# Identity products ahead of FFN, constants first, and a new order of the first FFN groups, in a fused retention and gated FFN kernel

## The chip, the cores and the metric

One core of a Trainium2 chip. The metric is device time in microseconds (us) for one execution. The kernel before takes 235.17 us in the median of its first 3 runs (234.81 to 235.84); lower is better. All tensors are fp32 in HBM; products run in bf16 with fp32 accumulation.

## The reference

```python
# retention: a decaying state per head; B=4, H=8, S=768, D=64
gamma = 1 - 2.0 ** (-5 - arange(H)); scale = 1 / sqrt(D)
for t in range(S):
    state = gamma * state + einsum('bhd,bhe->bhde', k[:, :, t], v[:, :, t])
    y[:, :, t] = scale * einsum('bhd,bhde->bhe', q[:, :, t], state)
# FFN: 3072 tokens, 512 -> 1536 -> 512
x = y.transpose(0, 2, 1, 3).reshape(B * S, H * D)
out = (1 / (1 + exp(-(x @ w_gate))) * (x @ w_val)) @ w_out
```

## The kernel before

Retention is computed in chunks of 128 tokens; FFN takes them in six blocks of 512 tokens (`xT[t]` is the transposed input of block t). Block 0 needs chunks 0 to 3, which are computed ahead as two "runs" of two chunks each. This opening takes some 27 us; after it, TensorE alternates FFN groups with pieces of later chunks. The schedule is written by hand, which fixes the order of each engine's instructions. Parts:

```python
def load_run(x, a, dtype, eng, name):       # one buffer per name: v's second load (vr) reuses the first's
    t = const.tile([128, H, 2 * D], dtype, name=name, tag=name, bufs=1)
    eng.dma_start(out=t, in_=...)
def scale_v(g, eng):                        # "L189": v times a table
    eng.tensor_tensor(vs[g], vf[g], tabv[...], op=ALU.mult)
def y_out_run(g):                           # "xT": VectorE writes a chunk's columns of FFN's input
    nc.vector.tensor_tensor(xT[0][:, :, cols]..., y[g]..., tab_y(g)..., op=ALU.mult)
def up(t, n1, lo=0, hi=512):                # 4 products with w_gate, 4 with w_val; hT = sigmoid * value
    ...
def keep_on(n):                             # identity products: no use but to keep TensorE busy
    u = bank([128, 512])
    for _ in range(n):
        nc.tensor.matmul(u[:, :128], ident, ident, start=True, stop=True)
# ... (cut) the opening:
scale_run(0, nc.vector)                     # vsr[0] = v * table
vr[1] = load_run(v, 1, F32, nc.sync, "vr")
# ...
keep_on(24)
transpose_run(kr[0], kT[0], [nc.scalar])    # k of run 0
state_run(0); state_out(0, zz[0]); sum_run(0); sum_run(1)
transpose_run(qr[0], qT[0], [nc.scalar, nc.vector])
state_out(1, za[1])
scores_run(0); masks_run(0, 0); masks_run(0, 1)
transpose_run(kr[1], kT[1], [nc.scalar])
inter_run(0); inter_run(1)
transpose_run(qr[1], qT[1], [nc.scalar])    # q of run 1
# ... (cut) second table, loads
intra_run(0); y_out_run(0); y_out_run(1)    # first xT pair
scores_run(1); masks_run(1, 0)
state_run(1); sum_run(2); state_out(2, za[2])       # sum_run(2): "the second sum"
masks_run(1, 1); sum_run(3)
inter_run(2)
up(0, 0, 0, 256); up(0, 1, 0, 256)
inter_run(3); intra_run(1)
y_out_run(2); y_out_run(3)                  # second xT pair
state_out(3, za[3])
up(0, 2, 0, 256); up(0, 3, 0, 256)
up_columns(0, range(0, 2), 256, 512); up_columns(0, range(2, 4), 256, 512)
# ... (cut) and in the steady part, near 64 us:
scale_v(12, nc.gpsimd); scale_v(13, nc.gpsimd)      # while scale_v(8..11) are VectorE's
```

Of the kernel before, what the change touches and what calls it, by code (L numbers as in the profile page):

```python
# [9 lines left out]
F32 = mybir.dt.float32  # L10
BF16 = mybir.dt.bfloat16
I32 = mybir.dt.int32
AX = mybir.ActivationFunctionType
ALU = mybir.AluOpType
# [3 lines left out]
def kernel(  # L18
# [10 lines left out]
    nc = tc.nc  # L29
    B, H, S, D = q.shape  # L30
# [53 lines left out]
    def load_gate_val(s):  # L84
        cols = slice(s * 256, (s + 1) * 256)
        for dst, w in ((wg, moe_w_gate), (wv, moe_w_val)):
            nc.gpsimd.dma_start(out=dst[:, :, cols],
                                in_=w.rearrange("(kk p) n -> p kk n", p=128)[:, :, cols])
# [34 lines left out]
    lgh = const.tile([128, H], F32, name="lgh")  # L123
    for h in range(H):
        nc.vector.memset(lgh[:, h:h + 1], -lg[h])
    tabr = const.tile([128, 2, H, 2], F32, name="tabr")
    nc.vector.tensor_tensor(tabr, tokr.unsqueeze(2).to_broadcast([128, 2, H, 2]),
                            lgh.unsqueeze(1).unsqueeze(3).to_broadcast([128, 2, H, 2]), op=ALU.mult)
    nc.scalar.activation(tabr, tabr, AX.Exp)
    tabv = const.tile([128, NCH, H], F32, name="tabv")  # L130
    nc.vector.tensor_tensor(tabv, tokv.unsqueeze(2).to_broadcast([128, NCH, H]),
                            lgh.unsqueeze(1).to_broadcast([128, NCH, H]), op=ALU.mult)
    nc.scalar.activation(tabv, tabv, AX.Exp)
    lgp = const.tile([128, NP], F32, name="lgp")
    lsc = const.tile([128, 1], F32, name="lsc")
    nc.vector.memset(lsc, math.log(scale))
# [6 lines left out]
    zbd = [const.tile([128, NP, C], BF16, name=f"zbd{i}") for i in range(4)]  # L143
    for t in zbd:
        nc.vector.memset(t, 0.0)
    taby = {c: const.tile([128, NP, n * C], F32, name=f"taby{c}") for c, n in ((0, 2), (2, 1), (3, 1), (4, 2))}

    def tab_y(c):
        first = c if c in taby else c - 1
        return taby[first][:, :, (c - first) * C:(c - first + 1) * C]  # L150

    def make_taby(c):
        n = taby[c].shape[2]
        for p in range(NP):
            nc.scalar.activation(taby[c][:, p, :], toky[:, c * C:c * C + n], AX.Exp, scale=lgp[:, p:p + 1], bias=lsc)

    def extend_taby(c):
        nc.gpsimd.tensor_tensor(tab_y(c), tab_y(c - 3), gup.unsqueeze(2).to_broadcast([128, NP, C]), op=ALU.mult)
# [8 lines left out]
    def bank(shape, dt=F32):  # L167
        return pf.tile(shape, dt, tag="ff", name="ff")
# [254 lines left out]
        row = t * 512 + sm * 128  # L423
        nc.sync.dma_start(out=out[row:row + 128, :], in_=ob)

    def keep_on(n):
        u = bank([128, 512])
        for _ in range(n):
            nc.tensor.matmul(u[:, :128], ident, ident, start=True, stop=True)

# [20 lines left out]
    vr[1] = load_run(v, 1, F32, nc.sync, "vr")  # L451
    load_gate_val(2)
    scale_run(1, nc.gpsimd)
    extend_taby(3)
    for s in range(3, NFF // 2):
        load_gate_val(s)
    keep_on(24)
    kT[0], qT[0], kT[1], qT[1] = (new_run_T() for _ in range(4))
    transpose_run(kr[0], kT[0], [nc.scalar])
    state_run(0)  # L460
    state_out(0, zz[0])
    sum_run(0)
    sum_run(1)
    transpose_run(qr[0], qT[0], [nc.scalar, nc.vector])
    state_out(1, za[1])
    scores_run(0)
    masks_run(0, 0)
    masks_run(0, 1)
    transpose_run(kr[1], kT[1], [nc.scalar])
    inter_run(0)  # L470
    inter_run(1)
    transpose_run(qr[1], qT[1], [nc.scalar])
    make_taby(2)
    extend_taby(4)
    extend_taby(5)
    for s in range(4):
        load_out(s)
    for g in range(4, 8):
        load_chunk(g)
    nc.scalar.preload_act_table(AX.Sigmoid)  # L480
    intra_run(0)
    y_out_run(0)
    y_out_run(1)
    scores_run(1)
    masks_run(1, 0)
    state_run(1)
    sum_run(2)
    state_out(2, za[2])
    masks_run(1, 1)
    sum_run(3)  # L490
    inter_run(2)
    up(0, 0, 0, 256)
    up(0, 1, 0, 256)
    inter_run(3)
    intra_run(1)
    y_out_run(2)
    y_out_run(3)
    state_out(3, za[3])
    up(0, 2, 0, 256)
    up(0, 3, 0, 256)  # L500
    up_columns(0, range(0, 2), 256, 512)
    up_columns(0, range(2, 4), 256, 512)


    def ups(t):
# [88 lines left out]
```

## Time and profile before

The points in time, read from the timeline: "First down product" is the first product with `w_out`; from there to the end both kernels have the same instructions in the same order. "Down to down" is from it to the first such product of block 1.

| kernel before, profiled run | us |
|---|---|
| q's second load lands (q of run 1) | 11.43 |
| v's second load: starts, lands | 7.3, 13.05 |
| first xT pair | 14.82 to 16.18 |
| second sum ends; second xT pair ends | 17.68; 21.75 |
| first down product | 40.74 |
| down to down | 42.11 |
| span of the profile | 233.4 |

The span is 1.8 us shorter than the device time of the same run. TensorE is busy 95% of the span. The same four products of L308 follow each other at 0.107 us at 12.49 and at 0.056 at 16.05. "Half clock" or "cold" and "full clock" or "warm" are here only names for the two, and "release" for the moment at which the first gives way to the second: 14.2 us in the kernel before. The column of the granted clock reads 1.00 on both sides of it. In the views of the profile PE is TensorE, PEld its weight loads, DVE VectorE, ACT ScalarE, POOL GpSimd and SP SyncE; L189 is line 189 of the kernel; a bracket says how long the engine stood idle before and what ended it.

### The profile page before, as it was taken

What the parts mean: (1) busy time and instruction counts of PE and PEld (TensorE: products, weight loads), DVE (VectorE), ACT (ScalarE), POOL (GpSimd) and SP (SyncE); (2) the same over time, 40 slices, a digit from 0 to 9 for tenths busy, and PEclk for the clock granted to TensorE, in tenths of its full rate; (3) what the DMA queues carried; (4) which work ended last, traced back from release to release, by engine and by line L of the source; (5) the groups of instructions that cost most, each with busy time, mean ns of one, the idle gap of its engine ahead of it and who ended that gap; (6) DMA issues with size and microseconds to landing.
All of it is one profiled execution on the core that took longest, in us unless ns stands there. A gap on an engine that the chain in (4) does not pass through costs nothing.

```text
span 233.4 us, 4591 instructions
## 1 busy us (share of the span) xinstructions
PE 221.2 (95%) x1851; PEld 125.5 (54%) x1872; DVE 112.1 (48%) x214; ACT 90.8 (39%) x167; POOL 89.7 (38%) x110
## 2 busy tenths in 40 slices
PE   4696999999999999999999999999999999999994
PEld 4574744557889745445445445445445454444444
DVE  3577343355896762274923445716236711243301
ACT  5675333264727332353521432522532422433221
POOL 7999846999984839600923000000000000000000
PEclk9999999999999999999999999999999999999999
DMA  7999999999999999992592343001200011100022
GB/s 135 215 198 196 200 205 210 213 263 244 222 132 133 162 174 181 242 148 59 39 156 81 112 96 61 3 25 70 91 0 0 3 45 66 69 3 0 0 90 90
DMA packets 74196, 27.03 MB, mean 116 GB/s; under 512 B 59840, under 2 KB 69952, under 8 KB 74176
## 3 DMA queue, kind: packets, MB, share of 16 engines
q0 software_dynamic: 55296, 16.26, 68.1%
q1 hardware_dynamic: 18736, 10.43, 19.1%
q8 instruction: 14, 0.23, 0.4%
q10 hardware_dynamic: 144, 0.07, 0.1%
q14 instruction: 6, 0.05, 0.1%
HBM read 28.31 MB, written 6.29 MB: 148 GB/s over the span
## 4 chain that ended last, share of the span: by engine, by line
PE 87%; DVE 4%; issue 3%; DMA 2%; ACT 2%; DVEq 0%; POOLq 0%
PE ff L386 46%; PE ff L417 25%; PE ff L400 5%; PE ff L247 2%; DMA kr<-in_k_dram 2%; PE ff L198 2%; PE ff L210 2%; PE ff L177 1%; PE ff L268 1%; PE ff L437 1%; PE z L216 1%; ACT zbd L222 1%; DVE xT L345 1%; ACT gs L390 1%; PE ff L317 1%
## 5 line engine op out<-in xcount | busy, mean ns | idle before, releaser
L391 DVE TENSOR_TENSOR hT<-gs,ff 128x512 bf16<-128x512 f32 (+1 forms) x72 | 45.1, 634 | 66.5 <-PE ff L386 61.5
L386 PE MATMUL ff<-xT,wg 128*128 128x512 bf16 (+1 forms) x277 | 67.3, 358 | 1.7 <-DVE xT L345 1.2
L386 PE MATMUL ff<-xT,wv 128*128 128x512 bf16 (+1 forms) x287 | 67.7, 358 | 0.4 <-DVE stA L299 0.3
L390 ACT ACTIVATE gs<-ff 128x512 f32<-128x512 f32 (+1 forms) x72 | 39.8, 556 | 69.3 <-PE ff L386 62.2
L417 PE MATMUL ff<-wo,hT 128*128 128x512 bf16 x267 | 61.1, 379 | 0.9 <-issue 0.5
L386 PEld LDWEIGHTS <-wv 128*128 128x128 bf16 x288 | 28.1, 98 | 28.8 <-DVE stA L299 0.6
L417 PEld LDWEIGHTS <-hT 128*128 128x128 bf16 x276 | 26.3, 98 | 31.3 <-DVE hT L391 0.6
L386 PEld LDWEIGHTS <-wg 128*128 128x128 bf16 x288 | 27.1, 98 | 28.7 <-issue 1.6
L422 ACT COPY ob<-ff 128x512 f32<-128x512 f32 x23 | 13.5, 586 | 48.9 <-PE ff L417 40.2
L255 DVE TENSOR_TENSOR xT<-ff,taby 128x512 bf16<-128x512 f32 x20 | 12.9, 685 | 23.5 <-PE ff L247 23.5
L189 POOL TENSOR_TENSOR vs<-vf,tabv 128x512 bf16<-128x512 f32 x12 | 12.8, 1090 | 25.3 <-PE ff L247 21.5
L62 POOL DMA_DIRECT2D vf<-in_v_dram x20 | 18.4, 919 | 5.2 <-DVE hT L406 2.7
L67 POOL DMA_DIRECT2D kn<-in_k_dram x20 | 18.3, 916 | 3.5 <-PE ff L400 1.1
L68 POOL DMA_DIRECT2D qn<-in_q_dram x20 | 18.1, 907 | 3.0 <-DMA wo<-in_moe_w_out_dram 2.5
L222 ACT CAST zbd<-za 64x256 bf16<-64x256 f32 x38 | 15.3, 403 | 9.0 <-DVE za L234 8.0
L203 DVE TENSOR_TENSOR stA<-ff,causal 128x512 bf16<-128x512 f32 x20 | 13.6, 679 | 0.0
L204 DVE TENSOR_TENSOR stB<-ff,causal 128x512 bf16<-128x512 f32 x20 | 13.6, 678 | 0.0
L179 ACT ACTIVATE qkT<-ff 128x1024 bf16<-128x1024 bf16 x8 | 8.2, 1026 | 1.6 <-PE ff L177 1.6
L400 PE MATMUL ff<-xT,wv 128*128 128x256 bf16 x56 | 7.3, 273 | 0.0
L400 PE MATMUL ff<-xT,wg 128*128 128x256 bf16 x56 | 7.3, 273 | 0.0
L189 DVE TENSOR_TENSOR vs<-vf,tabv 128x512 bf16<-128x512 f32 x8 | 7.0, 880 | 0.3 <-DMA vf<-in_v_dram 0.3
L406 DVE TENSOR_TENSOR hT<-gs,ff 128x512 bf16<-128x512 f32 x7 | 4.7, 684 | 4.6 <-PE ff L400 3.4
(85 smaller groups left out, 159.9 us busy)
## 6 DMA issues: line engine op xcount, KB each, us to landing
out_dram<-ob SPq DMA_DIRECT2D x23, 256.0 KB, 2.0
vf<-in_v_dram POOLq DMA_DIRECT2D x20, 256.0 KB, 7.2
kn<-in_k_dram POOLq DMA_DIRECT2D x20, 128.0 KB, 6.9
qn<-in_q_dram POOLq DMA_DIRECT2D x20, 128.0 KB, 6.8
wg<-in_moe_w_gate_dram POOLq DMA_DIRECT2D x6, 256.0 KB, 7.6
wv<-in_moe_w_val_dram POOLq DMA_DIRECT2D x6, 256.0 KB, 8.2
wo<-in_moe_w_out_dram POOLq DMA_DIRECT2D x4, 384.0 KB, 10.9
vr<-in_v_dram SPq DMA_DIRECT2D x2, 512.0 KB, 5.0
```

Of the source, the lines that this page charges most:

```text
L62: nc.gpsimd.dma_start(out=vf[g], in_=src(v, g))
L67: nc.gpsimd.dma_start(out=kn[g], in_=src(k, g))
L68: nc.gpsimd.dma_start(out=qn[g], in_=src(q, g))
L189: eng.tensor_tensor(vs[g], vf[g], tabv[:, g % NCH, :].unsqueeze(2).to_broadcast([C, H, D]), op=ALU.mult)
L203: nc.vector.tensor_tensor(stA[g], sc[g][0], causal4, op=ALU.mult)
L204: nc.vector.tensor_tensor(stB[g], sc[g][1], causal4, op=ALU.mult)
L222: nc.scalar.copy(zbd[g % 4][half, :, half], z[half])
L386: nc.tensor.matmul(u[:, lo:hi], w[:, kk, n1 * 128:(n1 + 1) * 128], xT[t][:, kk, lo:hi], start=(kk == 0), stop=(kk == KT - 1))
L390: nc.scalar.activation(gs[:, lo:hi], ps[0][:, lo:hi], AX.Sigmoid)
L391: nc.vector.tensor_tensor(hT[t][:, n1, lo:hi], gs[:, lo:hi], ps[1][:, lo:hi], op=ALU.mult)
L400: nc.tensor.matmul(u[:, i * n:(i + 1) * n], w[:, kk, n1 * 128:(n1 + 1) * 128], xT[t][:, kk, lo:hi], start=(kk == 0), stop=(kk == KT - 1))
L417: nc.tensor.matmul(o, hT[t][:, n1, sm * 128:(sm + 1) * 128], wo[:, n1, :], start=(n1 == 0), stop=(n1 == NFF - 1))
```

## The change

Its intent: bring TensorE to full clock earlier and keep it there by filling every wait ahead of FFN with identity products, free VectorE and ScalarE a little earlier, and put half-width FFN groups where TensorE would otherwise be idle.

```diff
@@ VectorE's constants: the tables, which wait for GpSimd's index tile, go behind the fills
-    tabr = ...; tabv = ...
     lgp, lsc, gup, zbd fills
+    tabr = ...; tabv = ...
@@ the opening
-    keep_on(24)
+    make_taby(2, range(2))            # half of the second table, rest below
+    warm = bank([128, 512])
+    keep_on(44, warm)
     transpose_run(kr[0], kT[0], [nc.scalar])
     state_run(0)
-    state_out(0, zz[0])               # ScalarE's casts: now behind its copy of q
     sum_run(0)
     sum_run(1)
+    keep_on(10, warm)
     transpose_run(qr[0], qT[0], [nc.scalar, nc.vector])
+    state_out(0, zz[0])
     state_out(1, za[1])
+    keep_on(12, warm)
     scores_run(0)
@@ (cut: rest of the table; loads and extend_taby moved behind y_out_run(1))
+    keep_on(10)
     scores_run(1)
     masks_run(1, 0)
+    inter_run(2)
+    keep_on(24)
     state_run(1)
     sum_run(2)
     state_out(2, za[2])
     masks_run(1, 1)
     sum_run(3)
-    inter_run(2)
     up(0, 0, 0, 256)
-    up(0, 1, 0, 256)
     inter_run(3)
     intra_run(1)
     y_out_run(2)
     y_out_run(3)
+    up(0, 1, 0, 256)
     state_out(3, za[3])
-    up(0, 2, 0, 256)
-    up(0, 3, 0, 256)
     up_columns(0, range(0, 2), 256, 512)
-    up_columns(0, range(2, 4), 256, 512)
+    up(0, 2)
+    up(0, 3)
```

More of the change, by code (lines that the diff above doesn't have):

```diff
@@ L125 @@
         nc.vector.memset(lgh[:, h:h + 1], -lg[h])
-    tabr = const.tile([128, 2, H, 2], F32, name="tabr")
-    nc.vector.tensor_tensor(tabr, tokr.unsqueeze(2).to_broadcast([128, 2, H, 2]),
-                            lgh.unsqueeze(1).unsqueeze(3).to_broadcast([128, 2, H, 2]), op=ALU.mult)
-    nc.scalar.activation(tabr, tabr, AX.Exp)
-    tabv = const.tile([128, NCH, H], F32, name="tabv")
-    nc.vector.tensor_tensor(tabv, tokv.unsqueeze(2).to_broadcast([128, NCH, H]),
-                            lgh.unsqueeze(1).to_broadcast([128, NCH, H]), op=ALU.mult)
-    nc.scalar.activation(tabv, tabv, AX.Exp)
     lgp = const.tile([128, NP], F32, name="lgp")
@@ L145 @@
         nc.vector.memset(t, 0.0)
+    tabr = const.tile([128, 2, H, 2], F32, name="tabr")
+    nc.vector.tensor_tensor(tabr, tokr.unsqueeze(2).to_broadcast([128, 2, H, 2]),
+                            lgh.unsqueeze(1).unsqueeze(3).to_broadcast([128, 2, H, 2]), op=ALU.mult)
+    nc.scalar.activation(tabr, tabr, AX.Exp)
+    tabv = const.tile([128, NCH, H], F32, name="tabv")
+    nc.vector.tensor_tensor(tabv, tokv.unsqueeze(2).to_broadcast([128, NCH, H]),
+                            lgh.unsqueeze(1).to_broadcast([128, NCH, H]), op=ALU.mult)
+    nc.scalar.activation(tabv, tabv, AX.Exp)
     taby = {c: const.tile([128, NP, n * C], F32, name=f"taby{c}") for c, n in ((0, 2), (2, 1), (3, 1), (4, 2))}
@@ L150, in tab_y, with make_taby @@
         return taby[first][:, :, (c - first) * C:(c - first + 1) * C]
-    def make_taby(c):
+    def make_taby(c, pairs=range(NP)):
         n = taby[c].shape[2]
-        for p in range(NP):
+        for p in pairs:
             nc.scalar.activation(taby[c][:, p, :], toky[:, c * C:c * C + n], AX.Exp, scale=lgp[:, p:p + 1], bias=lsc)
@@ L424, in down, with keep_on @@
         nc.sync.dma_start(out=out[row:row + 128, :], in_=ob)
-    def keep_on(n):
-        u = bank([128, 512])
+    def keep_on(n, u=None):
+        if u is None:
+            u = bank([128, 512])
         for _ in range(n):
@@ L453 @@
     scale_run(1, nc.gpsimd)
-    extend_taby(3)
-    for s in range(3, NFF // 2):
-        load_gate_val(s)
-    keep_on(24)
+    make_taby(2, range(2))
+    warm = bank([128, 512])
+    keep_on(44, warm)
     kT[0], qT[0], kT[1], qT[1] = (new_run_T() for _ in range(4))
@@ L469 @@
     transpose_run(kr[1], kT[1], [nc.scalar])
+    make_taby(2, range(2, 4))
     inter_run(0)
@@ L472 @@
     transpose_run(qr[1], qT[1], [nc.scalar])
-    make_taby(2)
+    nc.scalar.preload_act_table(AX.Sigmoid)
+    intra_run(0)
+    y_out_run(0)
+    y_out_run(1)
+    extend_taby(3)
+    for s in range(3, NFF // 2):
+        load_gate_val(s)
     extend_taby(4)
@@ L479 @@
         load_chunk(g)
-    nc.scalar.preload_act_table(AX.Sigmoid)
-    intra_run(0)
-    y_out_run(0)
-    y_out_run(1)
+    keep_on(10)
     scores_run(1)
     masks_run(1, 0)
+    inter_run(2)
+    keep_on(24)
     state_run(1)
```

## The prediction

> **What bounds the kernel now.** I read the busy shares first, then the stretches before the steady part, then the chain that ended last, then the timeline of the first 28 us.
>
> ```profile
> PE 221.2 (95%) x1851; PEld 125.5 (54%) x1872; DVE 112.1 (48%) x214; ACT 90.8 (39%) x167; POOL 89.7 (38%) x110
> ```
>
> TensorE is busy nearly all the time, so only its idle or slow time can be won. The view of stretches says where that lies (columns: stretch, length, busy us of PE, PEld, DVE, ACT, POOL with counts, then granted clock, DMA share, GB/s):
>
> ```profile
> 0.00:10.00 10.00, 5.37 (x88) 4.76 (x89) 4.05 (x33) 5.78 (x11) 8.56 (x20) 1.00 1.20 152
> 10.00:20.00 10.00, 8.48 (x208) 6.46 (x211) 8.23 (x17) 7.76 (x15) 9.85 (x13) 1.00 1.41 217
> 20.00:30.00 10.00, 8.73 (x90) 6.32 (x80) 4.40 (x8) 3.31 (x8) 8.32 (x10) 1.00 1.42 199
> ```
>
> About 7.4 of TensorE's 12 idle us lie in these 30 us, which hold the first four chunks of attention ("the runs") and the start of FFN. From up(0,4) on, in the kernel before the first full-width group, at 26.93 us, both kernels have the same instructions in the same order. Hence the method: find when TensorE starts that group after the change; the difference to 26.93 is the difference of the whole time, unless a later DMA eats it.
>
> The clock column says 1.00 throughout, but durations contradict it (timeline: start, us, engine, line, operation, count, idle before and releaser):
>
> ```profile
> 3.03 2.74 PE L429 MATMUL ff<-ident 128*128 128x128 bf16 x24 [3.03 <-POOL ident masks.py:199]
> ...
> 6.79 1.07 PE L268 MATMUL ff<-ident,kr 128*64 128x128 bf16 x16 [1.02 <-DMA kr<-in_k_dram]
> ...
> 12.49 0.61 PE L308 MATMUL ff<-qkT,zbd 128*128 128x128 bf16 x4
> ...
> 16.05 0.40 PE L308 MATMUL ff<-qkT,zbd 128*128 128x128 bf16 x4
> ```
>
> Less some 0.29 us of drain, 24 identity products took 2.45 us, 23 spacings of 0.1065. The same four products of L308 took 0.61 us at 12.49 and 0.40 at 16.05: spacings of about 0.107 and 0.056. In between, at 14.2, single products of L317 fall from 0.31 to 0.22 us. So TensorE ran at half clock until about 14.2 us. That, and the idle time, is what the new identity products aim at.
>
> The waits of the other engines there:
>
> ```profile
> 9.57 0.60 ACT L273 ACTIVATE qkT<-ff 128x512 bf16<-128x512 bf16 x1
> ...
> 9.58 0.42 DVE L336 COPY za<-z 128x256 f32<-128x256 f32 x1 [2.32 <-ACT zbd L222]
> ...
> 14.82 1.36 DVE L345 TENSOR_TENSOR xT<-ff,taby 128x512 bf16<-128x512 f32 x2 [1.36 <-PE ff L317]
> ...
> 17.27 0.41 DVE L338 TENSOR_TENSOR za<-za,z 128x256 f32<-128x256 f32 x1
> ...
> 20.41 1.34 DVE L345 TENSOR_TENSOR xT<-ff,taby 128x512 bf16<-128x512 f32 x2 [0.26 <-PE ff L317]
> ...
> 21.80 0.49 PE L386 MATMUL ff<-xT,wg 128*128 128x256 bf16 x3 [1.22 <-DVE xT L345]
> ```
>
> q's copy and the state sum stand behind ScalarE's casts (the cast pair begins at 8.82); VectorE then waits 1.36 us for slow TensorE; the last xT product of the runs ends at 21.75 and only then FFN can flow. The chain that ended last goes the same way: k's DMA to 6.75, the transposes, ScalarE, VectorE's masks, xT, then TensorE to the end.
>
> [...]
>
> **The change part by part.**
>
> *Constants first.* VectorE's 8 lgp fills (0.115 apart), 8 gup fills (0.85 in all) and four zbd fills (1.09) now run from 1.13 us, while it idled for GpSimd's index tile. They end near 4.05 instead of 6.18; the tables follow by 4.4, and vsr of run 0 starts when v lands (5.1) instead of 6.11. It is not on the path: its user, the state products, waits for k. v's second load reuses the buffer, so it goes at 6.3 instead of 7.3; but GpSimd issues weights until 13.04 anyway, so vsr of run 1 gains only 0.15. ScalarE's first two parts of the second table (0.82) fit into its idle 1.26 before 7.90. Worth: nearly nothing.
>
> *44 products instead of 24.* At 0.1065 they would end at 7.7, while k is there at 6.75. If the clock is released at W, the rest go at 0.056. With W = 6.5 the transposes start at 7.15, with W above 7.7 at 7.72: a loss of 0.35 to 0.9 against 6.79.[...]
>
> *To the masks, W = 6.5.* Transposes warm take 0.65 instead of 1.07: 7.8. ScalarE copies to 8.8; state products end 8.05; ten identity products (0.56) to 8.6; q's transposes to 9.25; ScalarE's half of q 9.25 to 9.85 and VectorE's half, which waits for it, to 10.3. Scores start at 9.9, and the first mask at 10.4 (before: 10.97). The twelve products lie in this wait and cost nothing. Four masks at 0.605 end at 12.85. Before, TensorE was still transposing, cold, when the masks ended at 13.46; now it waits for the last mask, the products of run 0 end at 13.35, and the xT pair runs 13.4 to 14.75 instead of 14.82 to 16.18: 1.4 won.
>
> *To the second sum.* ScalarE becomes the bound: from 9.85 it has four casts (1.64), k's copy (1.02), half a table (0.82), q's copy (1.02), with gaps to 14.45. Scores of run 1 start at 14.5 instead of 15.21: the win shrinks to 0.7. Masks end 16.2. But TensorE now does inter (0.3) and 24 identity products (1.35) before the state products: they end about 17.15, and the sum is at 17.35 instead of 17.27. VectorE idles some 1.1 us; the win is gone.
>
> *To FFN.* After the sum end: two masks 1.2, second sum 0.45, one hT product 0.45 (two before), xT pair 1.36, with gaps 3.5. Before it was 21.75 - 17.68 = 4.07, because inter of chunk 3 waited for ScalarE's gate in a shared buffer. So 0.55 is won. But the first-half group of up(0,1) has moved behind xT, and in the built program its second product waits for the last xT: 8 x 0.109 = 0.87, less one product already done, comes back onto TensorE. The work after xT is 0.77 + 16 x 0.109 + 16 x 0.2157 = 5.97 instead of 26.93 - 21.80 = 5.13, so 0.8 is lost.
>
> Sum for W = 6.5: the second sum ends 17.77, xT 21.25, the common group starts at about 27.25: +0.3. With W = 8.1 all of the opening is cold and the path is about 0.65 later: +0.95. With W = 9.8, +1.5; with W = 5.8, about zero. Mean about +0.6.
>
> **Rivals.** (1) The clock comes early and the products lie in real waits: the 24 must then hide behind GpSimd's vsr or the masks. For it: vsr of run 1 was ready only at 15.1. Against: the state products in the trace came after it at 15.65 without waiting. If GpSimd is 1 us later in the new kernel, the 24 cost nothing, and that is no gain either; a real gain needs the masks or ScalarE's copies faster than I list. It would give 233.5 to 234.5. (2) The opening shift is a pure loss: release late, everything before the scores cold and 0.9 late: 236.7. (3) A win in the first 27 us is hidden by DMA, because the next chunks are transfer-bound: the page shows DMA full to about 100 us. Against: k and q of chunk 5 land near 39 and are used at 46, four or more us in hand. So it would not eat 1 us.
>
> **Range and chances.** My list says 235.17 + 0.6 = 235.8. I shade it to 235.5, since the list adds every product as a delay, and an earlier release is what the longer opening is there to buy. The variants above span -1.5 to +1.7 round 235.2; I take 234.1 to 236.9 for 8 in 10. The change touches under 12% of the time and the whole idle time there is 7.4 us; 2% would be 4.7 us. So faster by over 2% has 0.02, within 2% 0.96, slower 0.02.
>
> **What would show it.** Right: first products of L317 at 0.22 us; masks of run 0 starting before 10.97; the first xT pair about 1 us earlier; ScalarE, not TensorE, releasing the scores of run 1; VectorE idle about 1 us before the sum near 17.3; TensorE idle while the second xT pair runs, then eight extra 256-wide products; the 512-wide group of up(0,4) starting 27 to 28. Wrong: the transposes of k starting at 6.8 already (release before 6), the state products of run 1 waiting for GpSimd, or up(0,1) running beside xT.

The four values of W (5.8, 6.5, 8.1, 9.8) were assumptions. The sum: about zero, +0.3, +0.95 and +1.5 for the four, taken together as about +0.6 (their even mean is 0.69), hence 235.17 + 0.6 = 235.8, shaded to 235.5. The wait of VectorE and GpSimd entered it as zero, since none lay on the chain of the kernel before.

## More of the kernel before

In the kernel before, q's second load (q of run 1) lands at 11.43 us. One more view of the kernel before is needed later, the timeline from 62 to 78 us, first VectorE's part (columns: start, us, engine, line, operation, count):

```profile
62.19 0.68 DVE L189 TENSOR_TENSOR vs<-vf,tabv 128x512 bf16<-128x512 f32 x1
...
63.84 0.88 DVE L189 TENSOR_TENSOR vs<-vf,tabv 128x512 bf16<-128x512 f32 x1
...
76.28 2.05 DVE L189 TENSOR_TENSOR vs<-vf,tabv 128x512 bf16<-128x512 f32 x1
```

GpSimd's part near 64 us, kernel before:

```profile
63.25 0.93 POOL L62 DMA_DIRECT2D vf<-in_v_dram  x1
64.16 2.47 POOL L189 TENSOR_TENSOR vs<-vf,tabv 128x512 bf16<-128x512 f32 x2
```

VectorE's first scaling took 0.68 us, the second 0.88, where GpSimd's two scalings of the same form began. The one at 76.28 took 2.05, beside another such pair of GpSimd (75.72 to 77.77); TensorE did not wait for it.

## The result, and the profile after

The changed kernel took 238.57 us in the median (237.84 to 238.84, 4 runs), the kernel before 235.41 in the same rounds (234.81 to 235.84, 4 runs). The ratio is 1.0131, 95% interval 1.0097 to 1.0165: inside the 2% band, but 1.7 us above the top of the predicted range. A ratio here is the mean time of one kernel's fast runs over that of the other's of the same rounds, so not quite the ratio of the medians quoted.

The changed kernel's busy shares:

```profile
PE 224.0 (95%) x1911; PEld 127.2 (54%) x1932; DVE 113.0 (48%) x213; ACT 90.9 (38%) x166; POOL 88.9 (38%) x110
```

Its first three stretches of 10 us, columns as in the prediction:

```profile
0.00:10.00 10.00, 6.97 (x116) 6.54 (x118) 4.48 (x34) 5.51 (x10) 8.56 (x21) 1.00 1.17 150
10.00:20.00 10.00, 8.48 (x236) 6.85 (x230) 7.11 (x14) 7.37 (x13) 8.45 (x11) 1.00 1.42 217
20.00:30.00 10.00, 8.17 (x79) 5.04 (x79) 4.46 (x8) 3.14 (x8) 9.25 (x12) 1.00 1.42 199
```

TensorE is busier in the first stretch (6.97 us for 5.37) and idler in the third (8.17 for 8.73): more products, less use. The changed kernel's timeline, TensorE:

```profile
7.84 0.82 PE L268 MATMUL ff<-ident,kr 128*64 128x128 bf16 x16
...
13.83 0.64 PE L268 MATMUL ff<-ident,qr 128*64 128x128 bf16 x16 [1.10 <-DMA qr<-in_q_dram]
...
16.44 1.50 PE L430 MATMUL ff<-ident 128*128 128x128 bf16 x24
...
20.10 0.22 PE L317 MATMUL ff<-stA,vsr 64*64 64x128 bf16 x1
20.90 0.21 PE L317 MATMUL ff<-stB,vsr 64*64 64x128 bf16 x1 [0.58 <-issue]
...
22.86 0.49 PE L386 MATMUL ff<-xT,wg 128*128 128x256 bf16 x3 [1.20 <-DVE xT L345]
```

The same timeline, VectorE:

```profile
11.51 0.69 DVE L299 TENSOR_TENSOR stA<-ff,maskr 128x512 bf16<-128x512 f32 x1
...
15.07 1.36 DVE L345 TENSOR_TENSOR xT<-ff,taby 128x512 bf16<-128x512 f32 x2 [1.08 <-PE ff L317]
...
18.36 0.42 DVE L338 TENSOR_TENSOR za<-za,z 128x256 f32<-128x256 f32 x1 [0.76 <-PE ff L329]
...
21.47 1.34 DVE L345 TENSOR_TENSOR xT<-ff,taby 128x512 bf16<-128x512 f32 x2 [0.82 <-PE ff L317]
```

Read them against the prediction's lines. The 24 products sit at 16.44 for 1.50 us. Two lines have no counterpart before: the transposes of q wait 1.10 us for q's DMA (not all of it lost, since the products behind also need the last mask, which ended at 13.99; in e11, e15 and e16, where nothing else held them, the first xT pair began 0.47 us after that mask, so here the wait cost some 0.6 there, an estimate), and in the middle of L317 (the products of run 1 with v) TensorE stands still, 0.58 us after the end of the product before, released by "issue", that is, by nothing that the profile shows. The chain of waits now runs over q, with a load of 8.44 us that was not on it before:

```profile
5.35 8.44 DMA qr<-in_q_dram
13.79 0.04 issue
13.83 0.64 PE ff L268 x16
```

A second loss lies far from the change. The changed kernel's timeline near 64 us, VectorE:

```profile
64.08 3.22 DVE L189 TENSOR_TENSOR vs<-vf,tabv 128x512 bf16<-128x512 f32 x1
67.22 0.74 DVE L391 TENSOR_TENSOR hT<-gs,ff 128x256 bf16<-128x256 f32 x2
```

The same place, GpSimd:

```profile
63.72 0.94 POOL L62 DMA_DIRECT2D vf<-in_v_dram  x1
64.64 2.10 POOL L189 TENSOR_TENSOR vs<-vf,tabv 128x512 bf16<-128x512 f32 x2
```

The scaling that takes 0.68 us takes 3.22 here, beside GpSimd's two. (It is the one that began at 62.19 before; FFN's delay of 1.9 us has moved it onto GpSimd's pair.) The products of hT behind it are late, and TensorE with them (its timeline):

```profile
67.69 0.38 PE L210 MATMUL ff<-qkT,zbd 128*128 128x128 bf16 x4 [1.67 <-DVE hT L391]
```

| point (us) | before | after | difference |
|---|---|---|---|
| v's second load: starts, lands | 7.3, 13.05 | 6.4, 13.97 | -0.9, +0.92 |
| q's second load lands | 11.43 | 13.79 | +2.36 |
| first xT pair begins | 14.82 | 15.07 | +0.25 |
| second sum ends | 17.68 | 18.79 | +1.11 |
| second xT pair ends | 21.75 | 22.81 | +1.06 |
| first down product | 40.74 | 42.63 | +1.89 |
| down to down | 42.11 | 43.86 | +1.75 |
| span | 233.4 | 237.0 | +3.6 |

So the loss is 1.89 before the common part and 1.75 near 64 us, 3.64 in all. The 1.89 is 1.06 up to the end of xT and 0.83 behind it.

### The profile page after: what moved, and what is told of

It is laid out like the page before. It is cut to its first block, busy times and chain, and to the rows that moved or that the text cites. A ratio compares the mean times of both kernels' runs of the same rounds, so it can differ in the third digit from the quotient of the medians.

```text
span 237.0 us, 4704 instructions
## 1 busy us (share of the span) xinstructions
PE 224.0 (95%) x1911; PEld 127.2 (54%) x1932; DVE 113.0 (48%) x213; ACT 90.9 (38%) x166; POOL 88.9 (38%) x110
## 3 DMA queue, kind: packets, MB, share of 16 engines
q0 software_dynamic: 55296, 16.26, 65.9%
## 4 chain that ended last, share of the span: by engine, by line
PE 86%; DVE 4%; DMA 4%; issue 3%; POOL 2%; ACT 0%; POOLq 0%; DVEq 0%
PE ff L386 46%; PE ff L417 24%; PE ff L400 4%; DMA qr<-in_q_dram 4%; PE ff L247 2%; PE ff L198 2%; PE ff L210 2%; PE ff L177 1%; PE ff L438 1%; DVE stB L204 1%; PE z L216 1%; PE ff L430 1%; DVE vs L189 1%; POOL kr L77 1%; DVE hT L391 1%
## 5 line engine op out<-in xcount | busy, mean ns | idle before, releaser
L391 DVE TENSOR_TENSOR hT<-gs,ff 128x512 bf16<-128x512 f32 (+1 forms) x72 | 45.6, 641 | 67.5 <-PE ff L386 63.1
L386 PE MATMUL ff<-xT,wg 128*128 128x512 bf16 (+1 forms) x277 | 68.2, 361 | 1.8 <-DVE xT L345 1.2
L390 ACT ACTIVATE gs<-ff 128x512 f32<-128x512 f32 (+1 forms) x72 | 40.5, 562 | 74.2 <-PE ff L386 65.9
L386 PE MATMUL ff<-xT,wv 128*128 128x512 bf16 (+1 forms) x287 | 68.6, 361 | 0.1
L430 PE MATMUL ff<-ident 128*128 128x128 bf16 x100 | 8.7, 261 | 3.0 <-POOL ident masks.py:199 3.0
L430 PEld LDWEIGHTS <-ident 128*128 128x128 bf16 x100 | 7.8, 120 | 3.3 <-POOL ident masks.py:199 3.0
L189 DVE TENSOR_TENSOR vs<-vf,tabv 128x512 bf16<-128x512 f32 x8 | 7.9, 1000 | 0.0
L210 PEld LDWEIGHTS <-zbd 128*128 128x128 bf16 x68 | 4.6, 98 | 4.0 <-issue 1.8
```

What stands on the lines that cost most here:

```text
L189: eng.tensor_tensor(vs[g], vf[g], tabv[:, g % NCH, :].unsqueeze(2).to_broadcast([C, H, D]), op=ALU.mult)
L386: nc.tensor.matmul(u[:, lo:hi], w[:, kk, n1 * 128:(n1 + 1) * 128], xT[t][:, kk, lo:hi], start=(kk == 0), stop=(kk == KT - 1))
L390: nc.scalar.activation(gs[:, lo:hi], ps[0][:, lo:hi], AX.Sigmoid)
L391: nc.vector.tensor_tensor(hT[t][:, n1, lo:hi], gs[:, lo:hi], ps[1][:, lo:hi], op=ALU.mult)
```

## The experiments

The theory at the start: (A) the opening loses by what was put on TensorE's path, the 24 products and the group moved behind xT; (B) q's second load is late because v's second load now starts ahead of the rest of it; (C) the loss at 64 us comes from VectorE's scaling meeting GpSimd's two (3.22 us for 0.68), set off by the shift. The rivals: the clash is a mere consequence of any delay; q's lateness is accident; TensorE's standstill within L317 is a wait that the profile doesn't show.

Seventeen kernels ran, all correct, all in 5 rounds. The kernel before gave medians of 235.34, 237.12, 235.84, 235.64 and 235.32 us on the five occasions, with single runs up to 240.45. Those have no trace; in four profiled runs of other kernels that were disturbed (e5, e13, e14, e17) loads of the opening landed late and TensorE fell back to half clock (mean granted clock of these runs 0.986, 0.986, 0.991 and 0.993). That noise is as large as what is sought, so the mechanisms are read from points in the traces, and the ratios serve as a second witness. "q" is the landing of q's second load, "sum" and "xT" the ends of the second sum and pair, "down" the first down product, "d-d" down to down.

| run | median us | ratio to before [95%] | q | sum | xT | down | d-d |
|---|---|---|---|---|---|---|---|
| e1 | 237.99 | 1.0090 [1.0039, 1.0142] | 11.43 | 18.79 | 22.84 | 42.67 | 43.51 |
| e2 | 238.42 | 1.0108 [1.0065, 1.0151] | 11.49 | 20.43 | 23.69 | 43.52 | 42.11 |
| e3 | 238.23 | 1.0137 [1.0081, 1.0193] | 12.0 | 17.89 | 21.97 | 41.80 | 42.10 |
| e4 | 238.52 | 1.0087 [1.0032, 1.0142] | 13.16 | 18.79 | 23.09 | 42.09 | 43.05 |
| e5 | 238.86 | 1.0095 [1.0016, 1.0174] | 11.89 | 18.80 | 24.98 | 44.98 | 42.11 |
| e6 | 238.61 | 1.0094 [1.0036, 1.0153] | 11.52 | 18.08 | 22.05 | 44.48 | 42.10 |
| e7 | 237.59 | 1.0048 [0.9962, 1.0133] | 12.15 | 17.57 | 21.86 | 40.85 | 42.10 |
| e8 | 236.05 | 1.0012 [0.9962, 1.0063] | 13.06 | 18.06 | 22.12 | 41.11 | 42.25 |
| e9 | 236.58 | 1.0019 [0.9964, 1.0073] | 13.07 | 18.68 | 21.93 | 41.76 | 42.10 |
| e10 | 237.32 | 1.0064 [1.0017, 1.0110] | 13.36 | 18.78 | 22.83 | 42.66 | 42.09 |
| e11 | 235.06 | 0.9961 [0.9919, 1.0003] | 11.35 | 17.40 | 21.04 | 40.03 | 42.10 |
| e12 | 235.36 | 0.9977 [0.9918, 1.0035] | 11.95 | 17.77 | 21.82 | 40.81 | 42.10 |
| e13 | 238.06 | 1.0054 [0.9997, 1.0110] | 14.88 | 22.62 | 25.87 | 45.69 | 42.11 |
| e14 | 235.41 | 0.9968 [0.9919, 1.0017] | 14.70 | 19.84 | 23.49 | 42.48 | 42.10 |
| e15 | 235.19 | 0.9969 [0.9914, 1.0023] | 11.83 | 17.66 | 22.28 | 40.40 | 42.11 |
| e16 | 233.62 | 0.9932 [0.9896, 0.9968] | 12.17 | 17.45 | 21.11 | 38.71 | 42.10 |
| e17 | 233.73 | 0.9941 [0.9900, 0.9982] | 12.22 | 18.43 | 23.88 | 41.49 | 42.10 |

### One part undone at a time (e1 to e4)

**e1**, the constants in their old order:

```diff
+    tabr = ...; tabv = ...            # back ahead of lgp, gup, zbd
     lgp, lsc, gup, zbd fills
-    tabr = ...; tabv = ...
```

> The changed kernel with VectorE's constants in their old order. Theory (early transfer): with the constants first, v's second load starts at 6.4 instead of 7.3 us and takes bandwidth from the second load of q, which lands at 13.8 instead of about 11.5. Undone, q lands by 12, the scores of run 1 start near 14.6 instead of 15.63, FFN's group up(0,4) starts about 1.0 us earlier than the changed kernel's 29.0, and the time is 1.0 us less (237.5), or up to 2.7 less (235.8) if the late clash of VectorE and GpSimd at 64 us goes too. Rival (q is late because of the products or the weights): q still lands near 13.8 and the time stays at 238.5.

q landed at 11.43, as before. Yet the first xT pair began at 15.04 for 15.07: TensorE, no longer waiting for q, stood still at another place instead, within the first L317, for 0.78 us in its weight loads. So two bounds coincided there, and the removal of one gives nothing. (In e2, e3, e4 and e10 too the first xT pair began at 15.02 to 15.04, with q at 11.49 to 13.36.) What the other is, the comparison under e9 tells. The clash remained (2.87 us at 64.1).

**e2**, constants first, but v's second load held back, by four spare fills and a late read of its buffer:

```diff
     scale_run(0, nc.vector)
+    spare = const.tile([128, NP, C], BF16, name="spare")
+    for _ in range(4):
+        nc.vector.memset(spare, 0.0)
+    nc.vector.tensor_copy(spare[:, 0, 0:1], vr[0][:, 0, 0:1])
     vr[1] = load_run(v, 1, F32, nc.sync, "vr")
```

> The changed kernel with constants still first, but about 1.1 us of spare fills and one late read of v on VectorE behind the scaling of run 0, so that v's second load starts at 7.4 to 7.6 us again; nothing else moves. Theory (early transfer of v): q lands by 12 as in the run with the constants back, and the time is the same as there within 0.4 us. Rival (not v, but the weights, which GpSimd issues 0.5 us earlier when VectorE's scaling no longer meets its mask work): q still lands after 13 us and the time stays near 238.5.

v's load started at 8.2 and q landed at 11.49 with the constants still first. So it is v's earlier start that makes q late (13.79 with v from 6.4, 11.49 with v from 8.2; that v "takes bandwidth" from q is the theory's wording, and only the landings are shown), not the constants themselves, nor the weights, the rival, which GpSimd issued from 7.47 as in the changed kernel (7.48; before: 7.97). But v now landed at 17.42, the state products waited, and the second sum ended at 20.43: the wait had only moved.

The views by tile show how. Tile `vr`, kernel before: two issues, the second at 7.3 us.

```profile
L77 SPq DMA_DIRECT2D vr<-in_v_dram x2: 384/420/456, 0.8 to 7.3; - x2
```

The same line of the changed kernel: VectorE's scaling frees the buffer earlier, and SyncE issues at 6.4.

```profile
L77 SPq DMA_DIRECT2D vr<-in_v_dram x2: 383/420/456, 0.8 to 6.4; - x2
```

Tile `qr` in the changed kernel: the slower of q's two loads took 8.4 us from issue, for 6.1 before.

```profile
DMA to landing us min/median/max: 5.0/6.7/8.4
```

Nor did v gain by its early start: it landed at 13.97 for 13.05. Over all kernels, q landed at 12.0 to 14.9 where the constants come first and v's load is not held back (after, e3, e4, e8, e9, e10, e13, e14; seven of the eight at 13.06 or later), and at 11.35 to 12.22 in all others.

**e3**, without the 24 products ahead of the state products:

```diff
     inter_run(2)
-    keep_on(24)
     state_run(1)
```

> The changed kernel without the 24 products before the state products of run 1. Theory (they are a plain delay, vsr of run 1 being ready at 16.0): the state products start near 16.7 instead of 17.94, the second sum ends near 18.0 instead of 18.79, the time is 0.6 to 0.9 us less. Rival (they keep TensorE's clock up): the first products of FFN run at spacings of 0.21 us instead of 0.108 and the time is the same or longer.

The second sum ended 0.90 earlier and the first down product came 0.83 earlier; products of L317 stayed at 0.22 us, so the clock did not need the 24. The part that the prediction sized at 1.1 is confirmed within 0.2. From the second sum to the end of xT it took 4.08, no less than the changed kernel's 4.02; the reason comes under e9. The median did not show it (238.23, runs from 236.13 to 240.62).

**e4**, the FFN groups in their old order:

```diff
     up(0, 0, 0, 256)
+    up(0, 1, 0, 256)
     inter_run(3)
@@
-    up(0, 1, 0, 256)
     state_out(3, za[3])
+    up(0, 2, 0, 256)
+    up(0, 3, 0, 256)
     up_columns(0, range(0, 2), 256, 512)
-    up(0, 2)
-    up(0, 3)
+    up_columns(0, range(2, 4), 256, 512)
```

> The changed kernel with the up groups in the old order and widths. Theory: the eight 256-wide products of up(0,1) leave the stretch behind the last xT (0.87 us less there), but one more hT product (0.42 us) stands ahead of xT; the time is 0.3 to 0.8 us less. Rival (the order costs nothing because xT alone sets the start): no difference beyond 0.2 us.

From the end of xT to the first down product it took 19.00 us for 19.82, so 0.82 of the 0.83 came back; xT itself ended 0.28 later, since one group more lies ahead of it. Net 0.54. The clash remained (2.03 us; TensorE waited 0.88 for it).

### What makes the clash (e5, e6, e10, e12)

If any delay of FFN sets off the clash, products put into the kernel before must do it too. **e5** adds 18, **e6** 36:

```diff
     up_columns(0, range(2, 4), 256, 512)
+    keep_on(18)        # e6: 36
```

> The kernel before with 18 identity products (1.0 us) put in directly ahead of up(0,4), and nothing else. Theory (a later FFN falls onto GpSimd's clock-bound work at 64 us): a delay of 1.0 may still pass, so +1.0 us, or +2.7 if VectorE's scaling of v already meets GpSimd's two. Rival (a delay only shifts the rest): +1.0 exactly, and no VectorE scaling longer than 1 us near 63 to 66 us beyond what the kernel before shows.

> The kernel before with 36 identity products (2.0 us) ahead of up(0,4). Theory (clash by phase): VectorE's scaling of v near 64 us takes about 3 us instead of 0.7, as in the changed kernel, and the time is +3.5 to +4.0 us, not +2.0. Rival (the clash comes from something else in the change): +2.0 us and no long scaling.

e6's first down product was 3.74 later than that of the kernel before, more than the changed kernel's 1.89, and there was no clash: GpSimd's pair ran from 63.6 to 65.7 and had ended when VectorE began at 65.9 (0.69 us). e5, whose opening also was disturbed (v landed at 15.6), had a mild one: VectorE's 1.26 us from 66.43, with down to down unchanged at 42.11. So "a delay makes the clash" falls; it is the phase between the two engines. VectorE follows FFN, while GpSimd's pair ("clock-bound" in e5's text), which stands behind its DMA issues, began at 64.64 for 64.16, 0.48 later, where FFN came 1.89 later.

**e10** takes the meeting itself away: GpSimd's two scalings go to VectorE.

```diff
             if t == 1 and i == len(groups) - 4:
-                scale_v(12, nc.gpsimd)
-                scale_v(13, nc.gpsimd)
+                scale_v(12, nc.vector)
+                scale_v(13, nc.vector)
```

> The changed kernel with the scaling of v for chunks 12 and 13 given to VectorE instead of GpSimd; nothing ahead of FFN changes. Theory (VectorE's scaling at 64 us took 3.22 us because GpSimd's two ran then): no VectorE scaling over 1 us near 64, the stretch from the first down group of block 0 to that of block 1 takes 42.1 instead of 43.86 us, and the time is about 1.7 us less than the changed kernel's (236.8 on a quiet chip). Rival (VectorE was held by its input's transfer): the long scaling stays.

e10's VectorE at the same place:

```profile
64.10 0.68 DVE L189 TENSOR_TENSOR vs<-vf,tabv 128x512 bf16<-128x512 f32 x1
```

The scaling took 0.68 us at the same moment, and down to down went from 43.86 to 42.09, while everything up to the first down product stayed (42.66 for 42.63). That shows the 1.75. **e12** is the same edit in the kernel before, to see whether the 0.20 there cost anything or the two extra scalings on VectorE do:

> The kernel before with chunks 12 and 13 scaled by VectorE. Theory: the profiled run of before shows only 0.2 us of clash, so the median gains 0 to 0.3 us; if the slow tail of its runs (up to 240) comes from this clash, the tail shortens, otherwise it stays.

Neither does: 42.10 for 42.11, span 233.4 as before, ratio 0.9977 with 1 in its interval. Its runs still went up to 238.45, so this clash alone does not make the slow runs of the kernel before.

Seven of the traces have the meeting near 64 us. In these, VectorE's scaling ended a fixed time after the start or after the end of GpSimd's pair; they do not show which of the two it will be:

| kernel | VectorE starts, takes | GpSimd's pair starts, takes | VectorE ends after |
|---|---|---|---|
| before | 63.84, 0.88 | 64.16, 2.47 | start of the pair + 0.56 |
| e8 | 64.21, 1.23 | 64.89, 2.45 | start of the pair + 0.55 |
| e9 | 64.86, 0.85 | 65.14, 2.48 | start of the pair + 0.57 |
| after | 64.08, 3.22 | 64.64, 2.10 | end of the pair + 0.56 |
| e1 | 64.12, 2.87 | 64.37, 2.06 | end of the pair + 0.56 |
| e4 | 65.19, 2.03 | 64.59, 2.06 | end of the pair + 0.57 |
| e5 | 66.43, 1.26 | 65.04, 2.09 | end of the pair + 0.56 |

Either VectorE's scaling ended 0.55 to 0.57 us after the start of the pair, and then the pair took 2.45 to 2.48 us, or it ended 0.56 to 0.57 after the end of the pair, the second operation included, and the pair took 2.06 to 2.10. In the first five rows VectorE's recorded start is 0.25 to 0.68 us ahead of GpSimd's, and it ended early three times and late twice; in those five, GpSimd was still in the issue of v's load when VectorE began. What decides is not settled.

Twelve of the traces, the kernel before among them, have a second meeting of the same kind, between 72 and 82 us, which the first reading overlooked. All 13 scalings that took longer there (0.98 to 3.25 us for 0.68) ended 0.55 to 0.56 after the end of one of GpSimd's scalings; in e7 (76.39, 1.32 us) that was the first of two in a row, so it is not always the end of the second. None of them cost anything: TensorE had no wait over 0.16 us there, and down to down is 42.10 in e9 with 3.05 us at 74.32. So here the length of a stall did not tell its cost; what counted was whether TensorE waited for the hT product behind it, as it did at 67.69 in the changed kernel, for 1.67 us.

### Where TensorE stands still, and parts combined (e7, e8, e9)

**e7** undoes three parts at once, those of e1, e3 and e4, so that the 76 other identity products, the early copy of q and the split table remain. **e8** puts constants first into the kernel before, alone (the first hunk of the change).

> The changed kernel with three parts undone at once: constants back, no 24 products, up groups back. What stays are the 44, 10, 12 and 10 products, q's copy ahead of the casts, and the split table. Theory (the three parts are the loss): no late q, no clash, and 234 to 235.5 us, equal to the kernel before or up to 1 us faster. Rival (the products that stay, or the longer opening, are a loss too): 236 or more.

> The kernel before with the constants first, alone. Theory (early transfer): v's second load starts near 6.4, q's second load lands at 13 to 14 instead of 11.5, the transposes of q wait where they had none, and the time is 0.3 to 1.0 us more (more if FFN then meets the clash). Rival (only the products make q late): no wait for q, the time within 0.2 us of before.

e7's first down product came at 40.85, back to the 40.74 of the kernel before (span 233.4 in both). So those three parts carry the loss ahead of the common part, and what remains of the change is worth about nothing. (Its median, 237.59, says nothing: the kernel before had 237.12 in the same rounds.) In e8 q landed at 13.06, 1.63 later than before, and the first down product came 0.37 later. In the kernel before, TensorE reaches q's transposes only at 13.02, so the late q costs little there (a wait of 0.20). The 0.37 can't be put down to it: in that profiled run v also landed 1.06 later (14.11), so that its scaling was ready at 16.16 for 15.10, and TensorE stayed at half clock until 18.9 (its transposes of q took 0.314 us each up to 13.9, for 0.219 in e1). The changed kernel is ready for them at 12.73 (13.83 less the wait of 1.10) and waits.

e7 also still had standstills in TensorE's weight loads. I counted pairs of weight load and product from the program's start. In every kernel made from the changed one with its products 128 wide, a standstill comes ahead of weight load 224 or 352, or both, 128 pairs apart, whatever instruction happens to stand there. Weight loads of the second L317 in the changed kernel (timeline):

```profile
20.02 0.14 PEld L317 LDWEIGHTS <-vsr 64*64 64x64 bf16 x8
20.90 0.38 PEld L317 LDWEIGHTS <-vsr 64*64 64x64 bf16 x24 [0.74 <-issue]
```

In e4:

```profile
21.07 0.48 PEld L317 LDWEIGHTS <-vsr 64*64 64x64 bf16 x32 [0.77 <-issue]
```

In e7:

```profile
19.19 0.37 PEld L317 LDWEIGHTS <-vsr 64*64 64x64 bf16 x24
20.16 0.16 PEld L317 LDWEIGHTS <-vsr 64*64 64x64 bf16 x8 [0.60 <-issue]
```

In e3:

```profile
19.13 0.48 PEld L317 LDWEIGHTS <-vsr 64*64 64x64 bf16 x32
21.06 0.11 PEld L386 LDWEIGHTS <-wg 128*128 128x128 bf16 x2 [1.45 <-issue]
```

The changed kernel stops after 8 loads. e4 has one FFN group more ahead of them, 8 pairs, and stops after 0. e7 has that group and 24 products fewer, so 16 pairs fewer: it stops after 24. e3 has 24 fewer: after 32, and there the last product of L317 is held (19.55 to 20.92), for which xT waits. The place moves exactly as the count says, which I take to speak against a data dependency. From start to start the standstill took 0.85 us in the changed kernel (20.05 to 20.90) and 1.37 in e3 (19.55 to 20.92). Each of the five ends of a standstill that I compared with the DMA records (e1 at 14.74 and 20.94, e7 at 13.97 and 20.16, after at 20.90) came 1.4 to 1.6 us after a packet ended (13.28, 19.31; 12.60, 18.69; 19.42) on the queue that the page calls "q8 instruction" (15 packets, 0.25 MB in the changed kernel). So I read these gaps as TensorE waiting for its own instructions; that is an inference from the count and these times, for the profile says only "issue". The kernel before reaches pairs 224 and 352 only at 15.65 and 26.39 us, 2.69 and 6.43 after such packets (12.96, 19.96), and shows no such gap; e2, which gets to pair 352 late too, at 21.7, shows none there either.

**e9** tests it: the same fill time in a quarter of the instructions, 512 columns wide, 26 products for 100.

```diff
     def keep_on(n, u=None): ...
-            nc.tensor.matmul(u[:, :128], ident, ident, start=True, stop=True)
+            nc.tensor.matmul(u.rearrange("p (i n) -> p i n", n=128), ident,
+                             ident.unsqueeze(1).to_broadcast([128, 4, 128]), start=True, stop=True)
@@ counts
-    44, 10, 12, 10, 24
+    11, 3, 3, 3, 6
```

> The changed kernel with each identity product made 512 wide and their number cut to a quarter (11, 3, 3, 3, 6 for 44, 10, 12, 10, 24): the same TensorE time within 0.3 us, 74 fewer pairs of weight load and product in TensorE's instruction stream. Theory (TensorE runs out of instructions: in all five traces with the 128-wide products it stands still for 0.6 to 0.8 us ahead of its weight load number 352, wherever in the program that is, and often ahead of number 224): those gaps are gone or lie elsewhere with nothing waiting, the second xT pair ends about 0.6 us sooner after the second sum (3.4 instead of 4.0 us), FFN's first down group starts near 42.0 instead of 42.63. Rival (the gap belongs to the products of the second intra group themselves, a wait that the trace does not name): the gap of 0.6 us stays in the second intra group.

Its weight loads of the second L317:

```profile
19.91 0.48 PEld L317 LDWEIGHTS <-vsr 64*64 64x64 bf16 x32
20.48 0.11 PEld L386 LDWEIGHTS <-wg 128*128 128x128 bf16 x2
```

All 32 run through, as the theory wants it and the rival, a hidden wait of these products, does not. From the end of the second sum to that of xT it took 3.25 us for 4.02, and the first down product came 0.87 earlier, with the second sum ending nearly as before (18.68 for 18.79). There was still a gap ahead of load 224 (16.36 to 17.03), now in the identity products. The clash passed off mildly (0.85 us).

### A better kernel (e11, e13 to e17)

**e11** puts together what helped: constants in their old order, wide identity products (11, 3, 3, 3), no 24, FFN groups in their old order, GpSimd's scalings on VectorE. **e13** is only e9 with e10. **e14** is e11 with constants first.

> A version meant to beat both: q's copy ahead of the casts, split table, the four groups of identity products 512 wide (11, 3, 3, 3), no 24 products, old constants order, old up groups, chunks 12 and 13 scaled by VectorE. If the losses are the late q, the instruction gaps, the 24 products, the up order and the clash: first down group of block 0 at 39.7 to 40.3 against 40.74 of the kernel before, no clash, 234.0 to 234.9 us, 0.3 to 0.5% faster than before. If the clock's early release is worth nothing: equal to before.

> The changed kernel with 512-wide identity products (a quarter of the instructions) and with chunks 12 and 13 scaled by VectorE; order, 24 products' time and constants as in the changed kernel. Theory (instruction gaps and clash are the part that the prediction missed): first down group of block 0 near 41.8, 42.1 us from there to that of block 1, a profiled span near 234.3 and a ratio to before of 1.000 to 1.005. Rival (another loss remains): 1.008 or more.

> As the version meant to beat both, but with the constants first. Theory (v's early load delays q's second load, and with no instruction gap to hide it the delay is on the path): q lands at 12.5 to 14 instead of 11.4, the first xT pair ends 0.3 to 1.0 us later than 15.29, the first down group of block 0 at 40.2 to 40.9 instead of 40.03. Rival (q's landing has slack): 40.0 again.

e11 brought the first down product to 40.03, 0.71 ahead of the kernel before, and the ratio to 0.9961 with 1.0003 at the end of its interval: a gain in the trace, not one in the times. (It still stands still 0.70 us ahead of load 224, at 16.52.) e13's profiled run was a slow one (240.14 us, q at 14.88), so its points are not compared; its ratio is 1.0054, no better than e9's. In e14's profiled run q landed at 14.70, its transposes waited 2.38 us, TensorE fell back to half clock for some 3 us (granted clock of the run: 0.991) and the first down product came at 42.48. Whether that is the price of v's early load isn't shown, since single runs of kernels without it have late loads too; the ratios of e14 and e11, 0.9968 and 0.9961, can't be told apart.

The largest wait left in the opening is TensorE's 1.2 us beside the second xT pair (before: 21.80, [1.22 <-DVE xT]). FFN groups on the first 256 tokens need only the first pair, so they could run in it. **e15** tries it with `up(0, 2)`, its hT product kept behind xT:

```diff
     intra_run(1)
+    up_02 = up(0, 2, 0, 256, late=True)
     y_out_run(2)
     y_out_run(3)
+    up_02()
     state_out(3, za[3])
-    up(0, 2, 0, 256)
```

> As the version meant to beat both, with the first half of up(0,2) issued ahead of the second xT pair and its hT product after it. Theory (TensorE stands idle 1.2 us beside xT only because a group issued behind xT waits for it): its eight products run beside xT, the first down group of block 0 starts at about 39.2 instead of 40.03, the time is 0.7 to 0.8 us less, 0.5 to 0.8% faster than before. Rival (VectorE's one more hT product behind xT, or buffers, take it back): 40.0.

It failed: xT ended at 22.28 for e11's 21.04. In the built program VectorE's write of the second pair waits for the last product of `up(0, 2)` (it began at 20.94, after 1.09 us of waiting for it): the 256-column halves of one tile interleave row by row, so the stretches that the products read and that VectorE writes overlap. The dependency had turned round. **e16** gives block 0 two separate halves and moves two groups:

```diff
-            xT[0] = at.tile([128, NP, 512], BF16, tag="xT", name="xT")
+            xT[0] = at.tile([128, 2, NP, 256], BF16, tag="xT", name="xT")
@@ 512-wide groups of block 0 read both halves: xT[0][:, :, kk, :]
     intra_run(1)
+    later = [up(0, n1, 0, 256, late=True) for n1 in (2, 3)]
     y_out_run(2)
     y_out_run(3)
+    for finish in later:
+        finish()
     state_out(3, za[3])
-    up(0, 2, 0, 256)
-    up(0, 3, 0, 256)
```

> The version meant to beat both, with the tile xT of block 0 laid out in two halves of 256 tokens and the first halves of up(0,2) and up(0,3) issued ahead of the second xT pair (their hT products after it). Theory (the wait was only between the halves of one tile): no idle time of TensorE over 0.3 us beside xT, first down group of block 0 at 38.7 to 39.2 instead of 40.03, 0.8 to 1.0% faster than before. Rival (the 512-wide products over two pieces run slower, or buffers bind): 39.8 or more.

e16's TensorE (timeline):

```profile
19.64 0.61 PE L387 MATMUL ff<-xT,wg 128*128 128x256 bf16 x4
...
20.96 0.60 PE L387 MATMUL ff<-xT,wv 128*128 128x256 bf16 x4
21.40 1.04 PE L387 MATMUL ff<-xT,wg 128*128 128x256 bf16 x8
```

e16's VectorE (timeline):

```profile
19.75 1.36 DVE L345 TENSOR_TENSOR xT<-ff,taby 128x512 bf16<-128x512 f32 x2
```

No wait is left: 16 products run while VectorE writes xT from 19.75 to 21.11. The first down product came at 38.71, 1.32 ahead of e11's. The median is 233.62 us, the ratio 0.9932 [0.9896, 0.9968]: e16 beats both kernels, by a little less than the 0.8 to 1.0% forecast. **e17** is the kernel before with the halves and the two moved groups, and GpSimd's scalings on VectorE as in e12, without anything of the change:

> The kernel before with the same two halves and the same two early groups, nothing else. Theory: first down group of block 0 at 39.4 to 39.8 instead of 40.74, 0.4 to 0.6% faster than before; the identity products and the copies' order of the other version are then worth the difference of some 0.7 us. Rival (those are worth nothing): equal to the other version.

Its median is 233.73, ratio 0.9941 [0.9900, 0.9982]. So the halves carry nearly all of e16's gain; identity products and copy order add 0.1 us in the median, which these runs can't tell from none. Its profiled run was a disturbed one (v landed at 15.42, products at half clock from 18.29 to 20.85, four 256-wide ones in 1.06 us for 0.60, 235.93 us), so its points in the table say nothing of the halves.

## Why the prediction was wrong

Predicted 235.5, up to 236.9; measured 238.57. Taken by its own steps:

**The meeting of VectorE and GpSimd, put at zero: 1.75 us, the largest miss.** It was dismissed, because no such wait lay on the chain of the kernel before. But the trace had the two operations side by side, with 0.88 in place of 0.68 us at 63.84 and 2.05 at 76.28: the meeting was there, and off the chain by luck, at 63.84 because VectorE's scaling ended 0.56 us after the start of GpSimd's pair, not after its end. e10 shows the whole 1.75. Rival (3), which looked for a later event that would eat a gain, looked at DMA only. The premise that from the common group on "both kernels have the same instructions in the same order", so that the difference stays, is true of the instructions and failed for the time: GpSimd's pair moved by 0.48 us where FFN moved by 1.89.

**Constants first, "Worth: nearly nothing": the side effect was not looked for.** Its working has the mechanism, that v's second load goes at 6.3 (measured 6.4), and asks only what v gains. It didn't ask whose transfer it would delay. q landed 2.36 later, shown by e2 to come from v's start. The first xT pair, predicted "1.4 won" at 13.4 (about 14.05 with the release of the clock at 8.1), began at 15.07. Of these 1.0 us the masks, late by themselves, are some 0.4 and q's wait some 0.6 (the estimate above). e1 adds that q was not alone: without it the standstill at pair 224 held the same place, and undoing the constants gained nothing ahead of FFN (42.67 for 42.63). So what the late q cost in the changed kernel is not shown.

**"With gaps 3.5" from the second sum to the end of xT: measured 4.02.** e9 measured 3.25 for this stretch with the standstill gone, so the listed work was right or a little generous, and the term missing is 0.77 for TensorE's standstill. The prediction costed an identity product by its 0.056 us alone; 100 narrow ones are also 100 weight loads, and with 26 wide ones in their place the standstill on the path was gone.

**The clock: inside the predicted spread, its cost undersized.** From the transposes of k (0.82 us, between the 1.07 of the kernel before, cold, and the 0.64 that q's took later in the changed kernel, warm) the release came near 8.2, close to the variant with 8.1. So the aim was met: full clock some 6 us earlier than before (14.2), and from 5.6 to 8.2 us in all 13 kernels with the new opening. When it comes is not settled: with the old opening it was 14.2 to 14.7 in four kernels, about 6.4 in e5 and 18.9 in e8. (In the kernel before TensorE was busy for 3.28 of the 3.30 us before the release, and earlier, from 7.4 to 10.8, for 2.60 of 3.40 without one; whether that matters is not shown.) For the variant with 8.1 the prediction gave the common group at +0.95 for a measured +1.89. The transposes began at 7.84, predicted at most 7.72, and the steps up to the masks took longer than listed: the first mask came 1.11 later than with W = 6.5, not 0.65. Shown wrong with it: the masks at 10.4 (measured 11.51, later than the 10.97 before), and ScalarE as what releases the scores of run 1; on the chain ten identity products stood there, ending about when ScalarE's copy of the late q did (15.53); and the masks of run 1 waited for VectorE's own first xT pair until 16.33.

**Right.** The 24 products: about 1.1 predicted, 0.9 by e3. The new order of FFN groups: 0.8 predicted behind xT, 0.83 measured and 0.82 undone by e4. TensorE idle during the second xT pair, then the eight extra 256-wide products: as predicted. That the whole stays within 2%: it did.

The sum as it should have been: the predicted +0.95 for this release of the clock, +0.5 for the standstill, about +0.4 for the path to the second sum (18.79 for 17.77 + 0.65), +1.75 at 64 us: 3.6, the measured difference of the spans. How the 0.4 splits is not shown: the masks of run 0 were already 0.46 behind that variant (11.51 for 10.4 + 0.65), before q's second load or pair 224 could matter, and of q and the standstill at pair 224 e1 removed one and met the other. The rival nearest to the truth was (2), a pure loss at 236.7, though not for its reason, a late release.

Still open: what decides whether VectorE's scaling ends after the start or after the end of GpSimd's pair; what sets the moment of the clock's release; why in single runs (e5, e13, e14, e17) loads land several us later; and what TensorE waits for at pairs 224 and 352, which the profile does not name.

## What to carry to other kernels

Filler products had two costs here: without the 24 that stood ahead of work that had its operands the second sum came 0.90 us earlier (e3), and with 26 wide ones for all 100 narrow ones the path behind it was 0.77 shorter (e9). So use few and wide ones, and none ahead of such work. When a change frees a buffer earlier, ask what the transfer that then starts will delay; and when it shifts one engine's stream against another's, look through the whole trace for pairs of VectorE and GpSimd operations that pass each other closely, because here 0.20 us over the usual 0.68 became 2.54 over it; then ask whether TensorE waits for what stands behind it, since near 75 us up to 2.57 over it cost nothing. A wait is often better filled by real work, for which a layout may have to be split so that dependencies don't overlap: that alone gave what the identity products were meant to give.
